# Cross network on one core: a second Strassen level for product 4 in both tiles, the W block's residual by DMA, weight loads held by deadlines

## The chip, the core and the metric

The kernel runs on one core of one Trainium2 chip. The time is in device microseconds, from the start of the execution to its end. The kernel before took 2218.09 us (median of 3 runs, 2217.39 to 2218.19). The execution that the profiler recorded took 2217.99 us, 0.1 us under that median; its instructions span 2216.2 us.

## The reference

Six layers of a cross network on a batch of 16384 rows with 1024 features, all in bfloat16:

```python
B, F, D, L = 16384, 100, 16, 6          # Din = 1024
def reference(x0, ws, bs):
    x = x0
    for l in range(L):
        proj = jnp.einsum('bd,de->be', x, ws[l]) + bs[l]
        x = x0 * proj + x
    return x
```

So each layer is one product of the state with a 1024 x 1024 weight matrix, a bias, a multiplication with the input x0, and a residual addition to the state.

## The kernel before, in words

**Tiles and units.** The batch is cut into 16 tiles of 1024 rows (`pr`), worked on in 8 groups of two (`grp`). Within a group the two tiles take turns: layer 0 of the first tile (`lane` 0), layer 0 of the second (`lane` 1), layer 1 of the first, and so on. One tile in one layer is a *unit*; there are 96, and a name such as `T1@50` is operation T1 of unit 50. Features lie on the 128 partitions, rows on the free axis. A tile has four blocks of 512 features x 512 rows, so that a block is 128 partitions x 2048 elements (`QD`). The input is in `x0Ts`, the state in `xsts`, three of each: the tiles of one group use two, the third is the one that the next group's first tile will use.

**The product.** Each unit's 1024 x 1024 x 1024 product is made by the Winograd form of Strassen's method: seven products of 512 x 512 x 512, numbered 1 to 7, with four sums of the state's blocks (`T1` to `T4`) ahead of them and the sums of weight blocks (`5`, `6`, `7`, `3`) made once in group 0 and kept in device memory (`Lc`). A product can be done in two ways. *Plain* (`group`, matmul at line 318): 4 groups of 4 matmuls, each 128 x 128 weights by 512 columns, then 4 evictions from PSUM with bias by ScalarE (line 337). *With a second level* (`inner`, matmul at line 507): seven products of half the size, `Xp1` to `Xp7`, each 4 matmuls by 256 columns. For it VectorE makes sums of quarter blocks first (`Xt13`, `Xt2`, `Xt4` into `tin`), ScalarE does seven evictions without bias (`e_p5`, `f1`, `e_c11`, `f2`, `e_u0`, `e_u1`, `e_c21`, line 327), and VectorE adds the intermediate (`Xcc`). Products 5, 2 and 3 have the second level in nearly every unit. Product 4 has it where `lane in K4[l]`: in both tiles at layer 0, in the second tile alone at layers 1 to 4, in neither at layer 5. The first tile of group 0 (`one`) has it nowhere but for product 5, as its weight sums are only being made.

**After the products.** The results lie in seven blocks of SBUF, `ev` (`P1s`, `P5s`, `Q`, `U`, `V`, `W`, `C3`), which change places from unit to unit (`home`, `NEXT`). VectorE adds them up (`Q1`, `Ua`, `Ub`, `Va`; with the second level of product 4 also `Wa`, as then V has to be added to W), multiplies each of Q, U, V, W with its block of x0 (`Qm` to `Wm`), and the residual is added: at layers 1 to 4 by an accumulating DMA that GpSimd issues for Q, U and V (`Qx`, `Ux`, `Vx`; line 564, set by `DMA_RES`), and by a VectorE addition for W. In group 0 W goes by DMA too. At layer 5 all four are VectorE additions; at layer 0 the multiplication writes the state. Every VectorE operation is recorded by the one helper at line 204.

**Weights.** They stream through a ring of 12 buffers (`wring`, tiles `wp`). From group 1 on each layer loads 11 blocks of 512 KB (10 at layer 5), on SyncE's queue (line 247), in the order of `ring_seq`: three raw blocks from `ws` and the rest from `Lc`. `pump()` runs after every operation that is emitted and issues a load as soon as the buffer that it overwrites has had its last use. On the same queue go the transposing loads of x0 (line 342) and, for the output, a transpose out of the state (line 662) and a store (line 671).

**The order of the work.** TensorE's order in a unit is written out by hand, as one of the lists `PE_FIRST`, `PE_ONE5` (first tile of group 0), `PE_TWO` (product 4 plain), `PE_FOUR` (product 4 with the second level) and `PE_LAST`. The function `schedule` then places all other operations: it is a list scheduler with a fixed cost for each operation, which gives an engine the operation whose latest start is the earliest. Costs: a VectorE operation n/1920 + 0.068 us, an eviction 0.571 us with bias and 0.475 us without, an accumulating DMA `ACCUM` = 9.0 us until its block may be read. The instructions are emitted in that order; on the chip each engine runs its own list and waits on semaphores.

Of the kernel before, what the change touches and what calls it, by code (L numbers as in the profile page):

```python
# [9 lines left out]
ADD = mybir.AluOpType.add  # L10
# [6 lines left out]
PE_FIRST = """  # L17
t0.0 t0.1 t0.2 t0.3 P1.1 bT P1.0 t1.0 t1.1 t1.2 t1.3 P1.2 P1.3 t2.0 t2.1 P2.1 t2.2 t2.3 P2.0 P2.2 P2.3
P5.1 P5.0 P5.3 P5.2 P6.3 P6.2 P6.0 P7.3 P6.1 P7.0 P4.3 P7.2 P7.1 P4.0 P4.2 P4.1 P3.0 P3.1 P3.3 P3.2
""".split()  # L20
PE_ONE5 = """
P1.1 P1.0 P2.1 P6.0 P2.0 P1.2 5p5 5p1 P1.3 P6.1 5p2 P2.3 5p6 P6.2 P2.2 5p7 P6.3 5p3 P7.2 P7.3 5p4 P3.3 P7.1 P3.2 P7.0
P4.3 P4.2 P4.0 P3.1 P4.1 P3.0
""".split()
PE_TWO = """
5p5 P1.1 5p1 P1.0 P1.3 5p2 2p5 5p6 2p1 P1.2 5p3 2p2 5p7 2p6 P6.0 5p4 2p3 3p5 2p7 3p1 P6.1 2p4 3p2 3p6 P6.2 P6.3 3p3
3p7 P7.0 P7.1 P7.2 3p4 P7.3 P4.1 P4.0 P4.3 P4.2
""".split()
PE_FOUR = """
5p5 P1.0 5p1 2p5 2p1 P1.1 5p2 5p6 2p2 P1.2 2p6 P1.3 5p3 5p7 2p3 2p7 P6.0 3p5 5p4 2p4 P6.1 P6.3 3p1 4p5 P6.2 4p1 3p2  # L30
P7.0 4p2 3p6 4p6 P7.1 3p3 4p3 4p7 P7.2 3p7 4p4 P7.3 3p4
""".split()
PE_LAST = """
# [5 lines left out]

ACCUM = 9.0  # L40

# [84 lines left out]


@with_exitstack
def kernel(
# [7 lines left out]
    nc = tc.nc  # L137
    P = nc.NUM_PARTITIONS
    B, D = x0.shape
    L = ws.shape[0]  # L140
# [10 lines left out]
    NDUMMY = 8  # L151
    K4 = {0: (0, 1), 1: (1,), 2: (1,), 3: (1,), 4: (1,)}
    DMA_RES = {1: "QUV", 2: "QUV", 3: "QUV", 4: "QUV"}

# [20 lines left out]
    EV = {"5c": P5s, "3c": C3, "U": U, "V": V, "W": W, "Q": Q, "P1s": P1s}  # L175
    NEXT = {"5c": "3c", "3c": "5c", "U": "W", "V": "U", "W": "V", "Q": "Q", "P1s": "P1s"}
    home = {r: r for r in EV}
    TURNED, rows = ((0, 0), (1, 0), (0, 1)), (P1s, U, V)
# [42 lines left out]
    for gl in range(NGROUP * L):  # L221
        if gl < L:
            ring_seq += [(gl, w, "load") for w in RAW] + [(gl, w, "make") for w in MADE]
        else:
            ring_seq += [(gl, w, "load") for w in "1 5 5i 2 2i 6 3 3i 7 4 4i".split()[:11 if gl % L in K4 else 10]]
    slot = {(gl, w): f"slot{i % RING}" for i, (gl, w, _) in enumerate(ring_seq)}
# [11 lines left out]

    def pump():
        while pos["next"] < len(ring_seq):  # L240
            gl, w, kind = ring_seq[pos["next"]]
            if kind == "make":
                return
            t = ring_tile((gl, w))
            if t is None:
                return
            nc.sync.dma_start(t[:], w_src(gl % L, w))
            pos["next"] += 1
# [29 lines left out]
    for u, (pr, l) in enumerate(units):  # L278
        one, first, last = plain(u), u == 0, u == NU - 1
        if not first:  # L280
            home = {r: home[NEXT[r]] for r in home}
        P1s, P5s, Q, U, V, W, C3 = (EV[home[r]] for r in ("P1s", "5c", "Q", "U", "V", "W", "3c"))
        CB = {"5": P5s, "2": Q, "3": C3, "4": W}
        gl, grp, lane = gl_of(u), pr // 2, pr % 2
        x0T, xst = x0Ts[pr % 3], xsts[pr % 3]
# [7 lines left out]
        ISW = [ISN[w] for w in ISLOT] + [f"is.{w}.{i}" for w in ISLOT for i in "5637"] if pr == 2 else []  # L293
        line = {w: i for i, w in enumerate(PE_FIRST if first else PE_LAST if last else PE_ONE5 if one else PE_FOUR if lane in K4.get(l, ()) and pr > 0 else PE_TWO)}

# [3 lines left out]
        def act(name, fn, rd, wr, biased_=False, u=u, occ=None):  # L299
            occ = occ or (0.571 if biased_ else 0.475)  # L300
            op(f"{name}@{u}", "ACT", occ, occ + 0.17, fn, rd, wr)
# [11 lines left out]
        def group(name, w, bank, bname, rhs, rname, m, start, gl=gl, kmajor=kmajor):  # L313
            def fn():
                for k in range(KH):
                    r = rhs[:, k, :] if kmajor else rhs[:, :, k, :]
                    o = bank[:] if kmajor else bank[:].rearrange("p (j r) -> p j r", r=P)
                    nc.tensor.matmul(o, lhsT=wt[(gl, w)][:, k, m * P:(m + 1) * P], rhs=r,  # L318
                                     start=(start and k == 0), stop=(k == KH - 1), skip_group_check=True)
            if first and name in ("P5.0", "P5.1"):  # L320
                rname = rname + ["w0.5a"]
            else:
                rname = rname + wname(w)
            pe(name, 0.863, fn, rname, [bname], [w], at={"1": ARRIVE["w0.1"], "2": ARRIVE["w0.2"]}.get(w, 0.0) if first else 0.0)
# [25 lines left out]
        def fence(q, sp, u=u):  # L350
            def fn():
                nc.gpsimd.dma_start(seen[:], x0Ts[sp][0:1, q[1], q[0] * KH, 0:32])
            op(f"fence@{u}", "POOL", 0.6, 0.6, fn, [f"x0.{sp}.{q[0]}{q[1]}"], ["xbar"])

        if l == 0 and lane == 1:
# [121 lines left out]
        if inn:  # L477
            for X, a, b in (("5", 0, 1), ("2", 2, 3), ("3", 0, 1), ("4", 2, 3))[:len(inn)]:
# [12 lines left out]
                def inner(i, bank, start, X=X, gl=gl, q=q, tk=tk, src=src, kmajor=kmajor):  # L491
                    quad = {1: (0, 0), 2: (1, 0), 3: (1, 1)}
                    rhs = (lambda k: q(*quad[i], k)) if i in quad else (lambda k: tk({4: 3, 5: 0, 6: 2, 7: 1}[i], k))
                    rn = {1: src, 2: src, 3: src, 4: X + "t4", 5: X + "t13", 6: X + "t2", 7: X + "t13"}[i]
                    w = X if i in (1, 2, 4) else X + "i"

                    def fn():
                        if i in (1, 2, 4):
                            k0, e0 = {1: (0, 0), 2: (KQ, 0), 4: (KQ, HQ)}[i]
                            wv = wt[(gl, w)][:, k0:k0 + KQ, e0:e0 + HQ]  # L500
                        else:
                            wi = weight(gl, w) if gl < L else weight(gl, w)[:]
                            wv = wi.rearrange("p q (k e) -> p q k e", k=KQ)[:, {5: 0, 6: 1, 3: 2, 7: 3}[i]]
                        for m in range(KQ):
                            for k in range(KQ):
                                o = pX[bank][:, m * NQ:(m + 1) * NQ]
                                nc.tensor.matmul(o if kmajor else o.rearrange("p (j r) -> p j r", r=P), lhsT=wv[:, k, m * P:(m + 1) * P],  # L507
                                                 rhs=rhs(k), start=(start and m == 0 and k == 0), stop=(k == KQ - 1), skip_group_check=True)
                    if gl < L and w.endswith("i"):
                        dep, wl = [f"is.{w}.{({5: '5', 6: '6', 3: '3', 7: '7'})[i]}", ISN[w]], []  # L510
                    else:
                        dep, wl = ([] if X in "24" else wname(w)), [w]
                    pe(X + f"p{i}", 0.436, fn, [rn, Xn[bank]] + dep, [Xn[bank]], wl)
# [34 lines left out]
        if not last:  # L548
            if not one:
                ttop("Q1", Q[:], Q[:], P1s[:], ADD, allm("Q") + allm("P1s"), allm("Q"))  # L550
            ttop("Ua", U[:], U[:], P5s[:], ADD, allm("U") + allm("5c"), allm("U"))
            if not one:
                ttop("Ub", U[:], U[:], C3[:], ADD, allm("U") + allm("3c"), allm("U"))
            if "4" in inn:
                ttop("Wa", W[:], W[:], V[:], ADD, allm("W") + allm("V"), allm("W"))
            ttop("Va", V[:], V[:], P5s[:], ADD, allm("V") + allm("5c"), allm("V"))
            for nm, C, q in (("Q", Q, (0, 0)), ("U", U, (0, 1)), ("V", V, (1, 1)), ("W", W, (1, 0))):
                if l == 0:
                    ttop(nm + "m", xblk(xst, *q), C[:], x0j(*q), MULT, allm(nm) + [X0[q]], [XO[q]] + ISW)
                    continue  # L560
                ttop(nm + "m", C[:], C[:], x0j(*q), MULT, allm(nm) + [X0[q]], allm(nm))
                if nm in DMA_RES.get(l, "") or nm == "W" and grp == 0 and 0 < l < L - 1:
                    def acc(C=C, q=q, xst=xst):
                        nc.gpsimd.dma_start(xblk(xst, *q), C[:], accum_op=ADD)  # L564
                    op(f"{nm}x@{u}", "POOL", 1.0, ACCUM, acc, allm(nm) + [XO[q], "xbar"], [XO[q]])
                else:
                    ttop(nm + "x", xblk(xst, *q), C[:], xblk(xst, *q), ADD, allm(nm) + [XO[q]], [XO[q]])
        else:
# [7 lines left out]
            r0 = pr * PR  # L576
            END = NU * 22.95
            half = lambda s, h: [f"{s}.{2 * h}", f"{s}.{2 * h + 1}"]
# [95 lines left out]

    order, start, _ = schedule(ops)

    ctx.enter_context(tc.manual_schedule(
# [31 lines left out]

    held = [i for i in order if ops[i].name.startswith("ld") and ops[i].name.endswith(".1@1")]  # L710
    for i in held:
        ops[i].fn()
    for i in order:
        if i not in held:
            ops[i].fn()
        for k in ops[i].weights:
            if k in uses_left:
                uses_left[k] -= 1
        pump()

# [29 lines left out]
```

## Time and profile before

| | |
|---|---|
| median of 3 runs | 2218.09 us |
| the profiled execution | 2217.99 us, span 2216.2 us |
| TensorE (PE) busy | 2203.0 us, 99%, 14637 matmuls |
| VectorE (DVE) busy | 2143.7 us, 97%, 2539 instructions |
| ScalarE (ACT) busy | 2038.9 us, 92%, 3657 instructions |
| GpSimd (POOL) busy | 211.1 us, 10%; 200 accumulating DMAs |
| DMA queue q1 (SyncE's), q0 (GpSimd's) | 53.5% and 29.1% of the 16 DMA engines' time |

An engine's busy time is the union of its instructions' spans. A span holds the start of the pipeline and its end, so that two instructions that follow each other closely overlap by some 0.09 us; the step from start to start is then shorter than the duration that a row gives. The queues' shares are of the time of all 16 DMA engines over the span.

### The profile page before, as it was taken

How to read it: one execution, taken by the hardware profiler on the slowest of the kernel's cores; microseconds unless marked ns; L12 is line 12 of the kernel's file. 1: busy time of each engine (PE TensorE's matmuls, PEld its weight loads, DVE VectorE, ACT ScalarE, POOL GpSimd, SP SyncE). 2: the span in 40 equal slices, each digit the busy share in tenths (PEclk: the TensorE clock that was granted, in tenths of full speed). 3: DMA queues.
4: the chain of work that ended last, by engine and by line, in shares of the span. 5: the costliest groups of instructions: out<-in, count | busy, mean ns of one | idle time of the engine just before them, and what ended most of it. 6: DMA issues, size and time to landing. Idle time of an engine off the chain costs nothing.

```text
span 2216.2 us, 39701 instructions
## 1 busy us (share of the span) xinstructions
PE 2203.0 (99%) x14637; PEld 1432.6 (65%) x14685; DVE 2143.7 (97%) x2539; ACT 2038.9 (92%) x3657; POOL 211.1 (10%) x271
## 2 busy tenths in 40 slices
PE   9999999999999999999999999999999999999998
PEld 5555666666666666666666666666666666666664
DVE  8999999999999999999999999999999999999997
ACT  7888899999999999999999999999999999999997
POOL 1132100110001100011000110011100111001110
PEclk9999999999999999999999999999999999999999
DMA  8788999768986689866898678976789777896777
GB/s 257 208 222 239 215 239 263 182 171 216 259 254 176 177 226 252 256 173 179 237 251 237 172 197 226 261 222 177 214 224 251 216 181 224 214 272 185 201 224 166
DMA packets 455460, 482.88 MB, mean 218 GB/s; under 512 B 269152, under 2 KB 381280, under 8 KB 455264
## 3 DMA queue, kind: packets, MB, share of 16 engines
q1 hardware_dynamic: 418352, 349.49, 53.5%
q0 software_dynamic: 36320, 130.57, 29.1%
q8 instruction: 115, 1.88, 0.3%
q14 instruction: 81, 0.66, 0.1%
q10 hardware_dynamic: 592, 0.27, 0.0%
HBM read 252.72 MB, written 58.20 MB: 140 GB/s over the span
## 4 chain that ended last, share of the span: by engine, by line
PE 99%; SPq 0%; DMA 0%; issue 0%; DVE 0%; DVEq 0%
PE pA L318 52%; PE pX L507 44%; PE pX L318 2%; DMA x0T<-in_x_dram 0%; SPq L691 0%; PE pA L611 0%; SPq L698 0%; DVE T L204 0%; SPq L704 0%; PE pX L611 0%; DVE xst L623 0%; SPq L701 0%; DVEq L204 0%
## 5 line engine op out<-in xcount | busy, mean ns | idle before, releaser
L507 PEld LDWEIGHTS <-wp 128*128 128x128 bf16 x8484 | 829.8, 98 | 275.4 <-issue 1.0
L337 ACT ACTIVATE ev<-pA,b_all 128x512 bf16<-128x512 f32 x1291 | 881.6, 692 | 107.5 <-PE pA L318 66.3
L318 PE MATMUL pA<-T,wp 128*128 128x512 bf16 x3825 | 922.2, 379 | 1.6
L318 PEld LDWEIGHTS <-wp 128*128 128x128 bf16 x5648 | 552.0, 98 | 478.4 <-issue 2.1
L327 ACT CAST ev<-pX 128x512 bf16<-128x512 f32 x1284 | 699.5, 595 | 24.2 <-PE pX L507 21.1
L507 PE MATMUL pX<-ti,wp 128*128 128x256 bf16 x4768 | 661.2, 273 | 0.0
L204 DVE TENSOR_TENSOR ev<-ev,ev 128x2048 bf16<-128x2048 bf16 x419 | 503.4, 1219 | 43.9 <-ACT ev L327 35.8
L204 DVE TENSOR_TENSOR ev<-ev,x0T 128x2048 bf16<-128x2048 bf16 (+1 forms) x324 | 386.0, 1210 | 2.3 <-ACT ev L337 1.2
L327 ACT COPY pX<-pX 128x512 f32<-128x512 f32 x638 | 370.8, 593 | 3.6
L318 PE MATMUL pA<-xst,wp 128*128 128x512 bf16 x1280 | 320.5, 379 | 0.0
L564 POOL DMA_DIRECT2D xst<-ev x200 | 172.3, 862 | 1296.8 <-ACT ev L337 445.6
L507 PE MATMUL pX<-xst,wp 128*128 128x256 bf16 x1736 | 260.5, 273 | 0.0
L507 PE MATMUL pX<-T,wp 128*128 128x256 bf16 x1628 | 244.3, 273 | 0.0
L204 DVE TENSOR_TENSOR ev<-ev,ip 128x1024 bf16<-128x1024 bf16 x319 | 214.4, 690 | 0.0
L204 DVE TENSOR_TENSOR T<-xst,T 128x2048 bf16<-128x2048 bf16 x160 | 195.6, 1223 | 1.0 <-PE pX L507 1.0
L204 DVE TENSOR_TENSOR T<-xst 128x2048 bf16<-128x2048 bf16 x160 | 195.6, 1223 | 0.0
L327 ACT CAST ip<-pX 128x512 bf16<-128x512 f32 x319 | 187.8, 589 | 2.1 <-PE pX L507 2.1
L204 DVE TENSOR_TENSOR xst<-ev,xst 128x2048 bf16<-128x2048 bf16 x116 | 141.8, 1224 | 0.1
L204 DVE TENSOR_TENSOR ti<-T,ti 128x512 bf16<-128x512 bf16 x282 | 119.6, 424 | 0.0
L204 DVE TENSOR_TENSOR ti<-xst 128x1024 bf16<-128x1024 bf16 x148 | 102.3, 691 | 9.3 <-PE pX L507 8.3
L204 DVE TENSOR_TENSOR ti<-xst,ti 128x1024 bf16<-128x1024 bf16 x148 | 101.8, 688 | 0.1
L204 DVE TENSOR_TENSOR ti<-T 128x1024 bf16<-128x1024 bf16 x141 | 97.3, 690 | 0.0
(57 smaller groups left out, 702.7 us busy)
## 6 DMA issues: line engine op xcount, KB each, us to landing
wp<-Lc SPq DMA_DIRECT2D x329, 512.0 KB, 6.1
xst<-ev POOLq DMA_DIRECT2D x200, 512.0 KB, 5.3
wp<-in_ws_dram SPq DMA_DIRECT2D x148, 512.0 KB, 6.7
out_dram<-x0T SPq DMA_DIRECT2D x60, 512.0 KB, 4.3
Lc<-wp POOLq DMA_DIRECT2D x24, 512.0 KB, 5.9
Lc<-xst POOLq DMA_DIRECT2D x23, 512.0 KB, 8.9
ev<-in_x_dram SPq DMA_DIRECT2D x3, 512.0 KB, 6.5
wp<-in_ws_dram SPq DMA_DIRECT2D x4, 256.0 KB, 7.4
```

Of the source, the lines that this page charges most:

```text
L204: nc.vector.tensor_tensor(out=o, in0=a, in1=b, op=op)
L318: nc.tensor.matmul(o, lhsT=wt[(gl, w)][:, k, m * P:(m + 1) * P], rhs=r, start=(start and k == 0), stop=(k == KH - 1), skip_group_check=True)
L327: act(name, lambda: nc.scalar.copy(out=dst, in_=src), rd, wr)
L337: act(name, lambda: nc.scalar.activation(out=dst, in_=src, func=IDENT, bias=b_all[:, c:c + 1], scale=1.0), rd, wr, True)
L507: nc.tensor.matmul(o if kmajor else o.rearrange("p (j r) -> p j r", r=P), lhsT=wv[:, k, m * P:(m + 1) * P], rhs=rhs(k), start=(start and m ...
L564: nc.gpsimd.dma_start(xblk(xst, *q), C[:], accum_op=ADD)
```

## The change

- **Product 4.** `K4` now names both tiles for layers 0 to 4. The first tile takes the second level for product 4 at layers 1 to 4 as well (in groups 1 to 7).
- **W's residual.** `DMA_RES` is "QUVW" at layers 1 to 4: the VectorE addition `Wx` becomes an accumulating DMA in all groups.
- **The idle state tile.** In groups 1 to 7 the second tile's Q, U, V and W of layers 1 to 4 are no longer in `ev` but in the third state tile, which the next group's first tile does not need before its layer 0 (`S` names). An operation `lend`, which emits no instruction, puts this in order with the output transposes that read the tile before and with the writes of the next group's layer 0. The places in `ev` change by another cycle (`NEXT`).
- **Loads.** `LOAD_ORDER` replaces the order of the blocks in the ring. After scheduling, `plan_loads` gives each load of groups 1 to 7 a time: not before its buffer is free, laid out one after the other with 1.45 us a load and 2.9 us for each accumulating DMA that it lets pass, and no later than 7.0 us ahead of its first use (less where several are due in a row). `pump` holds a load until that time has come in the order of emission, and the load then waits for the newest matmul emitted by then.
- **Orders and costs.** `PE_ONE5` (now `PE_ONE_INNER`), `PE_TWO` and `PE_FOUR` are other permutations of the same entries; `Ua` is recorded after `Wa`; the costs are 0.583 and 0.482 us for evictions and 9.5 us for an accumulating DMA, and the due time of the last outputs is `NU * 22.8`.

```diff
-ACCUM = 9.0
+ACCUM = 9.5
+LOAD, BURST, LEAD, GRACE = 1.45, 2.9, 7.0, 4.0
+LOAD_ORDER = "1 5i 2i 5 2 6 3i 3 4i 4 7".split()
...
+def plan_loads(loads, bursts):
+    deadline, nxt = [0.0] * len(loads), 1e9
+    for n in range(len(loads) - 1, -1, -1):
+        nxt = min(nxt, loads[n][1] - LEAD)
+        deadline[n] = nxt
+        nxt -= 1.3 * LOAD
+    issue, t, b = [], 0.0, 0
+    bursts = [s + 1.0 for s in sorted(bursts)] + [1e9]
+    for (free, _), due in zip(loads, deadline):
+        while True:
+            t = max(t, min(free, bursts[b]))
+            if bursts[b] <= t and (free > t or bursts[b] + GRACE <= due):
+                t += BURST
+                b += 1
+            else:
+                break
+        issue.append(t)
+        t += LOAD
+    return issue
...
-    K4 = {0: (0, 1), 1: (1,), 2: (1,), 3: (1,), 4: (1,)}
-    DMA_RES = {1: "QUV", 2: "QUV", 3: "QUV", 4: "QUV"}
+    K4 = {l: (0, 1) for l in range(L - 1)}
+    DMA_RES = {l: "QUVW" for l in range(1, L - 1)}
...
-    NEXT = {"5c": "3c", "3c": "5c", "U": "W", "V": "U", "W": "V", "Q": "Q", "P1s": "P1s"}
+    NEXT = {"5c": "Q", "3c": "5c", "U": "V", "V": "W", "W": "U", "Q": "3c", "P1s": "P1s"}
...
-    def pump():
+    def pump(time=0.0):
         while pos["next"] < len(ring_seq):
             gl, w, kind = ring_seq[pos["next"]]
-            if kind == "make":
+            if kind == "make" or held.get((gl, w), 0.0) > time:
                 return
...
-            nc.sync.dma_start(t[:], w_src(gl % L, w))
+            ld = nc.sync.dma_start(t[:], w_src(gl % L, w))
+            if (gl, w) in held:
+                tc.add_manual_dep(ld.ins, newest["pe"].ins.name, mybir.DependencyInfo(mybir.DependencyClass.Sync, mybir.DependencyReason.DATA))
...
+        idle = (2 * grp + 2) % 3
+        home = dict(cycle)
+        if grp > 0 and lane and 0 < l and not last:
+            home.update({r: "S" + r for r in "QUVW"})
+        EV.update({"S" + r: xsts[idle][:, i // 2, i % 2] for i, r in enumerate("QUVW")})
...
+        if lane == 0 and (grp > 0 and l == 1 or grp > 1 and l == 0 or grp == NGROUP - 1 and l == L - 1):
+            state = pr % 3 if l == 0 else idle
+            op(f"lend@{u}", "POOL", 0.0, 0.0, lambda: None, (), [f"S{r}.{m}" for r in "QUVW" for m in range(KH)] + [f"xs.{state}.{a}{b}" for a, b in QD])
...
-                if nm in DMA_RES.get(l, "") or nm == "W" and grp == 0 and 0 < l < L - 1:
+                if nm in DMA_RES.get(l, ""):
...
+    plan = plan_loads([(free_at[ring_seq[n - RING][:2]], first_use[k]) for n, k in late_keys],
+                      [start[i] for i, o in enumerate(ops) if o.name[1:3] == "x@" and o.eng == "POOL"])
+    for (_, k), t in zip(late_keys, plan):
+        held[k] = t
...
-        pump()
+        pump(start[i])
```

## The prediction

> **What bounds the kernel now.** I read the page's busy times first, then who waited for whom on TensorE and VectorE, then the chain of waits with its starts, then a table by stretches, one stretch for the two units of a layer, in group 4 (layers 0 to 5), and last the DMAs' landing times. From the page:
>
> ```profile
> PE 2203.0 (99%) x14637; PEld 1432.6 (65%) x14685; DVE 2143.7 (97%) x2539; ACT 2038.9 (92%) x3657; POOL 211.1 (10%) x271
> q1 hardware_dynamic: 418352, 349.49, 53.5%
> q0 software_dynamic: 36320, 130.57, 29.1%
> PE 99%; SPq 0%; DMA 0%; issue 0%; DVE 0%; DVEq 0%
> L507 PEld LDWEIGHTS <-wp 128*128 128x128 bf16 x8484 | 829.8, 98 | 275.4 <-issue 1.0
> ```
>
> A busy PE alone proves nothing, since the ends of matmuls are modelled. But the waits of PE between 300 and 2150 us are an empty list, and the chain's starts show the pace (start, length, then the number of matmuls):
>
> ```profile
> 1220.92 4.32 PE pA L318 x20
> 1226.54 1.31 PE pX L507 x12
> ...
> 1266.49 4.32 PE pA L318 x20
> ...
> 1357.63 4.32 PE pA L318 x20
> ...
> 1380.61 4.32 PE pA L318 x20
> ```
>
> A plain matmul takes 4.32 / 20 = 0.216 us, a half-width one 1.31 / 12 = 0.1092 us. The runs of 20 end the units with a plain product 4: two units of layers 1 to 4 take 1266.49 - 1220.92 = 45.57 us, a unit of layer 5 takes 1380.61 - 1357.63 = 22.98 us. So the unit with product 4 in two levels takes 45.57 - 22.98 = 22.59 us. TensorE sets the end at every point; the others only have to keep up. How closely they do is in the stretches (span, busy PE, PEld, DVE, ACT, POOL, clock, DMA share, GB/s):
>
> ```profile
> 1111.40:1156.50 45.10, 44.79 (x314) 31.09 (x319) 45.10 (x55) 43.27 (x80) 0.51 (x1) 1.00 0.99 254
> 1156.50:1202.20 45.70, 45.70 (x311) 30.23 (x310) 45.47 (x55) 43.04 (x78) 3.48 (x4) 1.00 0.92 251
> 1202.20:1247.80 45.60, 45.60 (x311) 30.16 (x309) 43.89 (x52) 42.75 (x78) 5.13 (x6) 1.00 0.73 200
> 1293.40:1339.00 45.60, 45.60 (x310) 30.16 (x309) 43.90 (x52) 42.76 (x78) 5.16 (x6) 1.00 0.73 196
> 1339.00:1384.90 45.90, 45.90 (x298) 28.89 (x297) 44.65 (x50) 41.98 (x75) 2.24 (x3) 1.00 0.83 201
> ```
>
> The first line is the one to remember: at layer 0 both tiles already run product 4 in two levels, DVE has no gap at all, and PE keeps its pace (the missing 0.3 us are missing records; it waited for nothing). The granted clock is 1.00 throughout.
>
> **TensorE, the only gain.** Converted are the first tiles of groups 1 to 7 at layers 1 to 4: 28 units. Each loses 16 plain matmuls (16 x 0.216 = 3.456 us) and gets 28 half-width ones (28 x 0.1092 = 3.058 us): 0.40 us. The units' lengths say 22.98 - 22.59 = 0.39. I take 0.395 x 28 = 11.1 us; the ends are 10.9 and 11.2. The 336 more weight loads take 98 ns each, less than the 109 ns of the matmul that covers them, as in the 8484 of that row. New orders of the same entries cost TensorE nothing while no entry waits; the start (to the first dense stretch) and the tail do the same work as before.
>
> [...]
>
> **ScalarE.** Per converted unit four evictions with bias go and seven without come. In a dense piece the steps from start to start are 0.59 us (1234.83 to 1235.42) and 0.46 to 0.51 us; 28 x (7 x 0.48 - 4 x 0.59) = 28 us more, 2067 of some 2205. Per pair it comes to layer 0's 43.27 of 45.10, with PE unhindered. Cost 0.
>
> **VectorE.** Steps from start to start, from the timeline: three 2048-element operations take 1344.02 - 1340.62 = 3.40 us, so 1.135 each; 1024 elements take 0.60; 512 take 0.335 (the row's 0.424 less the same 0.09 of overlap). A converted unit adds 4t13 and 4cc (1.20), 4t2 and 4t4 (0.67) and Wa (1.135): 3.01 us, 84.3 in all. W's residual leaves VectorE in 56 units (two tiles, four layers, seven groups): -63.6. Net +20.7 us in a time that is 11.1 shorter: 2164.4 of 2205, 98.2%; idle time shrinks from 72.5 to 40.7. Per pair of layers 1 to 4: 43.9 + 3.01 - 2.27 = 44.6 of 45.2. Lower end of the cost: 0, as all of it lies beside PE (layer 0's line, which has the same list of operations). Upper end: all 72.5 us of idle time are forced by dependences and stay; then VectorE sets the end and the time grows by the 20.7. I take 0, because layer 0's line is the same work at the same rate, and it is entered there with the backlog of layer 5, which stays as it is (four VectorE residuals, 44.65 of 45.90).
>
> **W by DMA.** 56 more accumulating DMAs of 512 KB. Queue q0's 29.1% is 645 us for 200 of them and 50 plain ones; the plain ones at the pace of q1's 4 KB packets (1.42 us a block, by the packets) leave 2.87 us each. So +160 us: the DMA engines go from 83% to about 91%, and a pair of layers 2 to 4 from 0.73 to 0.73 + 2 x 2.87 / 45.4 = 0.86. Nobody waits for a share; T1, 2t13, T2 and 3t13 of the same tile's next unit wait for landings:
>
> ```profile
> DMA to landing us min/median/max: 4.5/5.3/11.7
> ...
> xst<-ev POOLq DMA_DIRECT2D x6, 512.0 KB, 4.8
> ...
> xst<-ev POOLq DMA_DIRECT2D x9, 512.0 KB, 6.3
> ```
>
> These are all 200; then one pair of layer 2 in group 4 with six; then 208 to 254 us, in group 0, where W goes by DMA already and eight saves of weights run beside it. Even there the median is 6.3, against the 9.5 us that the order of work now allows and the 9.0 that it allowed. On GpSimd nothing waits behind an accumulation but the next (0.86 us each, 48 us more of an engine at 10%). Lower end 0; upper end 11.7 - 9.5 = 2.2 us of wait in each of 56 units, less the 40 us of idle, +83 us. I take 0, from group 0's row, which is nearest in kind: four per unit, DMA share 0.90 there, 0.4 us of wait for a landing on VectorE, none on PE.
>
> [...]
>
> **Held loads.** No load is added. What changes is when it is issued: as late as 7.0 us ahead of its use where the DMA engines have no other cause to take it earlier, and it first waits for a group of 4 matmuls to end, which costs up to 0.86 us of that. SyncE is in order, so behind a held load wait the next load, the transposes of x0 and the outputs; and PE waits for the load. Rows:
>
> ```profile
> wp<-Lc SPq DMA_DIRECT2D x329, 512.0 KB, 6.1
> ...
> wp<-in_ws_dram SPq DMA_DIRECT2D x148, 512.0 KB, 6.7
> ...
> DMA to landing us min/median/max: 3.2/6.3/13.2
> ```
>
> The medians come from bursts: five loads issued between 1232.2 and 1236.1 landed from 1238.4 to 1244.8, one every 1.3 to 2.4 us, behind an accumulation. Laid out 1.45 us apart, with 2.9 us left for accumulations (both the trace's own 1.42 and 2.87), they should be nearer 3.2 to 6. Lower end 0; the upper end is a rival below. I take 0.
>
> **Idle state tile.** It adds no instruction. The second tile's evictions no longer write blocks that the first tile's accumulations read; ScalarE shows no wait for those now, so nothing is gained. A new wait is for the output transposes that empty that tile: the last is over by 1155.5 us in group 4 (GpSimd's fence), the second tile's layer 1 begins after 1179. Cost 0. `Ua` behind `Wa`: same work.
>
> **Sum.** 2217.99 - 11.1 = 2206.9 for an execution like the profiled one; the median of the runs stood 0.1 above it, so 2207.0.
>
> **Rivals.**
> *Held loads land late (slower).* At the 35 stretches of layers 1 to 5 in groups 1 to 7 the 7 us less up to 0.86 are all there is. If the worst load of each stretch lands 1.2 us late (8.2 us; about a tenth of the loads take that now), PE stops for it: 35 x 1.2 = 42, to 2249 us. It turns at 11.1 / 35 = 0.32 us a stretch. For it: today PE never meets a load, so the margin is untested. Against it: the spacing, and the shortest landing of 3.2.
> *The same, in part.* Some 0.1 to 0.2 us a stretch, or a few late landings of W: 3 to 7 us of the gain go, 2210 to 2214.
> *VectorE becomes the bound.* Its idle time stays at 72.5 us: 2218.0 + 20.7 = 2238.7. It turns where the idle time falls by less than 20.7, to 51.8. For it: 98.2%, and 44 us of today's idle time between 300 and 2150 us are waits, 34 of them for ScalarE's evictions. Against it: they come at some 1.2 us a stretch in layers 2 to 5, where VectorE runs ahead, and layer 0 has none.
> *Half-width matmuls are paced by their weight loads.* 98 ns under 109: the rows exclude it.
>
> **How the numbers follow.** A difference under 0.2% (4.4 us) can hardly be told from none here. Dense PE, 2206 to 2209: 0.72. Gain eaten in part: 0.11 (2209 to 2213.7). Late loads: 0.06 within 0.2%, 0.07 slower. VectorE bound: 0.04, slower. Paced by weight loads: none. So faster 0.83, same 0.06, slower 0.11. The range is 2205.5 (the 11.2 and a little less tail) to 2213.7; it leaves the last three cases out.
>
> **What would show it.** Right: 22.6 us for every unit of layers 1 to 4, still no waits of PE between 300 and 2150, DVE without gaps (about 45 of 45.2) in layers 1 to 4, 256 accumulations at line 564's successor with a median near 6 us, q0 at about 36%. Wrong: waits of the weight loads on `wp`, or of PE on `ti` and `T` with DVE waiting for the landing of `xst`.

## The result, and the profile after

The changed kernel takes 2299.36 us (median of 6 runs, 2292.77 to 2311.91) and the kernel before 2217.77 us (median of 6): a ratio of 1.0376, 95% interval 1.0342 to 1.0411. It is 81.6 us slower; 2207.0 us had been forecast. The profiled execution of the changed kernel took 2293.25 us, near the fast end of its runs; its instructions span 2291.4 us, 75.2 us more than the span of before. Against those 75.2 us the accounts below are made.

From the page of the changed kernel, its busy times, its two large queues and the chain's shares by engine:

```profile
PE 2212.4 (97%) x14973; PEld 1468.8 (64%) x15021; DVE 2173.3 (95%) x2623; ACT 2058.0 (90%) x3741; POOL 259.1 (11%) x327
q1 hardware_dynamic: 418352, 349.49, 54.2%
q0 software_dynamic: 44384, 159.94, 34.2%
PE 82%; DMA 11%; DVE 5%; issue 1%; ACT 1%; SPq 0%; POOLq 0%; ACTq 0%; DVEq 0%
```

Before, TensorE was 99% busy and 99% of the chain. Now DMAs are 11% of the chain and VectorE 5%: the end is set in many places by something that arrives late. TensorE's waits between 300 and 2150 us, an empty list before (what waited, for what: us in all, times, the longest):

```profile
PE pA L351 <- DMA wp<-Lc: 29.0, 18, 3.1
PE pX L544 <- ACT pX L360: 13.9, 12, 3.0
PE pX L544 <- DMA wp<-in_ws_dram: 8.8, 5, 3.5
PE pA L351 <- DVE T L228: 5.3, 2, 2.8
PE pX L544 <- ACT ev L370: 0.7, 1, 0.7
```

The weights (`wp`) come late most often, and ScalarE's evictions next. Group 4 by stretches, layers 0 to 4, with the columns of the table shown of before (span, busy PE, PEld, DVE, ACT, POOL, clock, DMA share, GB/s):

```profile
1146.20:1193.30 47.10, 45.21 (x317) 31.33 (x321) 47.10 (x56) 43.06 (x81) 0.50 (x1) 1.00 0.98 255
1193.30:1238.50 45.20, 45.20 (x323) 31.29 (x321) 44.96 (x56) 43.05 (x82) 4.33 (x5) 1.00 0.88 221
1238.50:1283.60 45.10, 45.10 (x322) 31.21 (x320) 44.89 (x56) 43.47 (x81) 6.87 (x8) 1.00 0.88 224
1283.60:1330.40 46.80, 45.44 (x323) 31.30 (x322) 45.98 (x56) 43.66 (x81) 6.88 (x8) 1.00 0.88 215
1330.40:1379.90 49.50, 46.98 (x323) 31.90 (x321) 44.91 (x55) 43.80 (x81) 6.91 (x8) 0.97 0.82 205
```

Layers 1 and 2 run as forecast: 45.1 to 45.2 us a stretch instead of 45.6, TensorE without a gap, 44.9 us of VectorE, a DMA share of 0.88. Layers 0, 3 and 4 of the same group do not: 47.1, 46.8 and 49.5. In the last the granted clock is 0.97. So the steady state that was forecast exists, and what costs is how often it is broken.

**One late load.** The chain of the changed kernel around 1580 us (start, length, what):

```profile
1576.68 1.75 PE pX L544 x16
1578.43 0.88 PE pA L351 x4
1579.32 9.75 DMA wp<-Lc
1589.12 1.04 PE pA L351 x4
```

On SyncE's timeline (start, time on the queue) this load was the fifth since 1571; on GpSimd's, two accumulations were issued within 1.3 us of it:

```profile
1571.08 6.10 SPq L273 DMA_DIRECT2D wp<-Lc  x3
1578.02 0.38 SPq L273 DMA_DIRECT2D wp<-in_ws_dram  x1
1579.32 0.32 SPq L273 DMA_DIRECT2D wp<-Lc  x1
```
```profile
1578.33 0.86 POOL L602 DMA_DIRECT2D xst<-xst  x1 [10.17 <-ACT ev L360]
1580.61 0.86 POOL L602 DMA_DIRECT2D xst<-xst  x1 [1.41 <-ACT ev L360]
```

Those accumulations landed after 8.9 and 9.7 us, the load after 9.75. TensorE wanted it 6.8 us after its issue and stood for 3.0 us.

**One late x0.** The second kind of stop is at layer 0. In the waits between 1425 and 1450 us one delay is handed on three times, from a transposing load of x0 to VectorE, to ScalarE and to TensorE:

```profile
DVE T L228 <- DMA x0T<-in_x_dram: 4.6, 1, 4.6
...
PE pX L544 <- ACT pX L360: 3.6, 2, 3.0
ACT ip L360 <- DVE ev L228: 3.3, 1, 3.3
```

VectorE waits there for the last of the first tile's four transposes, which was issued at 1417.67 and landed at 1425.73. SyncE's timeline ahead of it shows why it is late: the transposes hold the queue for 2 to 4.6 us each, and loads stand between them:

```profile
1403.84 7.17 SPq L375 DMA_TRANSPOSE x0T<-in_x_dram  x3
1412.21 0.33 SPq L273 DMA_DIRECT2D wp<-Lc  x1
1412.63 3.88 SPq L375 DMA_TRANSPOSE x0T<-in_x_dram  x1
1416.62 0.53 SPq L273 DMA_DIRECT2D wp<-Lc  x1
1417.23 0.38 SPq L273 DMA_DIRECT2D wp<-in_ws_dram  x1
1417.67 4.64 SPq L375 DMA_TRANSPOSE x0T<-in_x_dram  x1
```

The kernel before starts earlier: in six of seven groups it issues the first of these four 13.2 to 13.6 us ahead of the first `T1` of their tile, the changed kernel 9.2 to 10.1 us.

**The account.** I took every step from the start of one matmul to the start of the next and called what it has over 0.216 us (0.109 for half width) a stop, where that is over 0.25 us. Stops make 69.1 us: 46.0 on late loads (26 stops of 0.5 to 3.7 us), 17.4 behind ScalarE, 5.6 behind VectorE. Another 13.7 us go at half clock: 27 us with a granted clock of 0.50, in windows of 3.4 us, each about the end of a stop of 2.6 to 3.7 us. The part after the last product's matmul grew from 9.7 to 14.5 us (last section). What is left, span less stops, half clock and end:

| | span | stops | half clock | end | left |
|---|---|---|---|---|---|
| before | 2216.2 | 0.0 | 0.0 | 9.7 | 2206.5 |
| changed | 2291.4 | 69.1 | 13.7 | 14.5 | 2194.1 |

The difference in the last column is some 12 us; 11.1 were forecast for TensorE. In the versions with few stops (below) it is 10.7 to 11.4. The gain is there, and 88 us of other losses lie on it.

### The profile page after: what moved, and what is told of

Same layout as the page of the kernel before. It is cut to its first block, busy times and chain, and to the rows that moved or that the text cites. A ratio compares the mean times of both kernels' runs of the same rounds, so it can differ in the third digit from the quotient of the medians.

```text
span 2291.4 us, 40900 instructions
## 1 busy us (share of the span) xinstructions
PE 2212.4 (97%) x14973; PEld 1468.8 (64%) x15021; DVE 2173.3 (95%) x2623; ACT 2058.0 (90%) x3741; POOL 259.1 (11%) x327
## 3 DMA queue, kind: packets, MB, share of 16 engines
q1 hardware_dynamic: 418352, 349.49, 54.2%
q0 software_dynamic: 44384, 159.94, 34.2%
## 4 chain that ended last, share of the span: by engine, by line
PE 82%; DMA 11%; DVE 5%; issue 1%; ACT 1%; SPq 0%; POOLq 0%; ACTq 0%; DVEq 0%
PE pA L351 40%; PE pX L544 39%; DMA wp<-Lc 8%; PE pX L351 2%; DVE xst L228 2%; DMA wp<-in_ws_dram 2%; DVE T L228 1%; DVE ti L228 1%; DVE ev L228 1%; DMA x0T<-in_x_dram 1%; DMA xst<-xst 0%; ACT pX L360 0%; SPq L739 0%; DMA xst<-x0T 0%; ACT ev L370 0%
## 5 line engine op out<-in xcount | busy, mean ns | idle before, releaser
L351 PE MATMUL pA<-T,wp 128*128 128x512 bf16 x3377 | 847.2, 381 | 39.6 <-DMA wp<-Lc 32.7
L544 PE MATMUL pX<-ti,wp 128*128 128x256 bf16 x5216 | 723.1, 273 | 0.0
L370 ACT ACTIVATE ev<-pA,b_all 128x512 bf16<-128x512 f32 x883 | 603.7, 694 | 112.5 <-PE pA L351 84.0
L360 ACT CAST ev<-pX 128x512 bf16<-128x512 f32 x1148 | 644.3, 594 | 25.5 <-PE pX L544 13.3
L360 ACT COPY pX<-pX 128x512 f32<-128x512 f32 x694 | 394.5, 590 | 14.8 <-PE pX L544 11.4
L228 DVE TENSOR_TENSOR ev<-ev,ev 128x2048 bf16<-128x2048 bf16 (+1 forms) x283 | 338.9, 1209 | 19.2 <-ACT ev L370 11.9
L228 DVE TENSOR_TENSOR ev<-ev,x0T 128x2048 bf16<-128x2048 bf16 (+2 forms) x188 | 223.9, 1192 | 0.4
L370 ACT ACTIVATE xst<-pA,b_all 128x512 bf16<-128x512 f32 x296 | 203.6, 688 | 19.3 <-PE pA L351 9.1
L228 DVE TENSOR_TENSOR xst<-xst,ev 128x2048 bf16<-128x2048 bf16 x136 | 165.5, 1218 | 1.6 <-ACT ev L360 0.6
L228 DVE TENSOR_TENSOR xst<-xst,x0T 128x2048 bf16<-128x2048 bf16 x136 | 164.3, 1216 | 0.2
L602 POOL DMA_DIRECT2D xst<-xst x112 | 96.2, 859 | 550.7 <-ACT ev L360 343.9
```

The costliest lines, as they stand in the source:

```text
L228: nc.vector.tensor_tensor(out=o, in0=a, in1=b, op=op)
L351: newest["pe"] = nc.tensor.matmul(o, lhsT=wt[(gl, w)][:, k, m * P:(m + 1) * P], rhs=r, start=(start and k == 0), stop=(k == KH - 1), skip_ ...
L360: act(name, lambda: nc.scalar.copy(out=dst, in_=src), rd, wr)
L370: act(name, lambda: nc.scalar.activation(out=dst, in_=src, func=IDENT, bias=b_all[:, c:c + 1], scale=1.0), rd, wr, True)
L544: newest["pe"] = nc.tensor.matmul(o if kmajor else o.rearrange("p (j r) -> p j r", r=P), lhsT=wv[:, k, m * P:(m + 1) * P], rhs=rhs(k), sta ...
```

## The experiments

After the result three explanations stood against each other. By the first the deadline of 7 us is too short by itself. By the second the fourth accumulation a unit crowds the DMA engines, so that whatever is issued late, or behind others, lands late. By the third VectorE, at 98%, has no room left and makes the delays. The runs undo one part, do one part alone, or take work away from one suspect.

### One part at a time

The changed kernel with its loads issued as soon as their buffers are free, as before the change:

```diff
-    for (_, k), t in zip(late_keys, plan):
-        held[k] = t
+    held.clear()
```

> The changed kernel whole, but its loads are issued as before, as soon as their buffer is free; no load waits for a matmul. Theory A (holding the loads to some 7 us ahead of use is what costs): the waits of PE and of its weight loads on wp go, the clock stays at 1.00, and the time falls from 2299 to 2207 to 2214 us. Theory B (the 56 more accumulating DMAs load the DMA engines so that loads come late however they are issued): it stays at 2270 or more, with PE still waiting for wp.

Measured: 2284.08 us, ratio 1.029 (1.0269 to 1.031). The late loads are gone and the kernel is hardly faster, so neither theory holds as it was written. Its waits, of TensorE and then of VectorE (300 to 2240 us):

```profile
PE pX L544 <- ACT pX L360: 32.8, 29, 3.0
PE pX L544 <- DVE ti L228: 16.3, 19, 1.4
...
DVE ti L228 <- DMA xst<-ev: 41.0, 24, 3.7
DVE T L228 <- DMA x0T<-in_x_dram: 20.6, 6, 5.2
```

Now it is the accumulations that land late: VectorE waits 41.0 us for the state, 20.6 for x0. Loads issued early take the DMA engines' time ahead of them: the median landing of a load is 7.2 and 11.0 us (5.1 and 6.0 when held), and a tenth of the accumulations out of `ev` take over 11.3 us (8.4 when held). The same shortage shows at another place. And it reaches W itself: with the accumulations taken in the order in which the kernel issues them, 30.8 us of the waits for the state are for the first tile's W, whose accumulations in groups 1 to 7 land after 11.2 us in the median, where the order of work allows 9.5. The late x0 is here too, though no load is held.

The other two parts, each put alone into the kernel before. Held loads alone (`plan_loads`, `held` and `pump(start[i])` as in the change, the load order of before):

```diff
-        pump()
+        pump(start[i])
```

> The kernel before with nothing changed but the hold (the same rule, 7 us, its own order of loads). Theory A: stops on wp of some 0.5 us a layer or more though the accumulations are still 200: 2225 to 2260 us. Theory B: 2218 us, as the DMA engines have no more to do than before.

Measured: 2228.41 us, 1.0054 (1.0039 to 1.0069), with 9.4 us of stops, 8.7 of them on `wp`. So held loads are sometimes late even at three accumulations a unit, with a fifth of the stops of the changed kernel. It is not a test of the same margin, though. In the schedule that each kernel's own code makes, the 7 us rule puts 79 of the 455 held loads of the changed kernel less than 8 us ahead of their first use (the shortest 6.9), and here none (the shortest 8.7). W by DMA alone:

```diff
-    DMA_RES = {1: "QUV", 2: "QUV", 3: "QUV", 4: "QUV"}
+    DMA_RES = {l: "QUVW" for l in range(1, L - 1)}
```

> The kernel before with nothing changed but W's residual by DMA in all groups (256 accumulations, loads as early as before). Theory A: 2218 us, PE without waits, the DMA engines at some 90%. Theory B: loads and landings late, 2240 us or more.

Measured: 2231.26 us, 1.0061 (1.0045 to 1.0078). This moves 56 additions off VectorE, whose busy time falls from 2143.7 to 2092.5 us, and still the kernel is slower: 7.3 us of stops behind ScalarE, 4.2 us more at the end, and a wait that before did not have, all of it for the first tile's U, whose accumulations now take 8.9 us in the median instead of 7.2:

```profile
DVE T L204 <- DMA xst<-ev: 22.3, 27, 2.5
```

Alone, then, held loads cost 10.7 us, W by DMA 13.5, and product 4 gains 11.1 by the forecast: +13 us if they added up. Together they cost 81.6. No run has product 4, the order of the loads, the idle state tile or the new orders of work alone; but all of these are also in the version of 2215.93 us below, so by themselves they don't cost 80 us. The loss lies in how the parts meet. The late x0, too, comes neither with held loads alone nor with W by DMA alone: VectorE never waits for it in these two kernels.

### Is it the crowding?

The accumulations are cut to half their bytes, once with early loads and once with the 7 us of the change:

```diff
-                        nc.gpsimd.dma_start(xblk(xst, *q), C[:], accum_op=ADD)
+                        nc.gpsimd.dma_start(xblk(xst, *q)[:, 0:KQ], C[:, 0:KQ], accum_op=ADD)
```

> The changed kernel without the hold (2284 us), each accumulating DMA carrying only the first half of its block, so that half of every residual at layers 1 to 4 is left out; instructions and waits are the same. Theory B and E (crowded DMA engines, landings later than the order of work allows): landings back to some 4 to 6 us, 2206 to 2216 us, the rest being x0 at layer 0. Theory D alone (a full VectorE, whatever the landings): 2250 us or more.

> The changed kernel, loads held to 7 us as in it, but each accumulating DMA adds only the first half of its block (256 KB instead of 512; the other half of the residual is left out). It tells whether the loads of 7 us are late by themselves or through the accumulations. Theory D (the accumulations crowd the DMA engines): some 190 us of engine time go, more than W by DMA brought, and the 46 us of PE's stops on wp fall below 10; with the layer-0 stops that remain, 2225 to 2240. Theory M (7.0 us less the wait for a matmul is too little margin by itself, whatever runs beside it): stops on wp stay above 30 us, 2270 or more. The kernel of before with held loads at 7 us, three accumulations a unit, had 8.7 us of them.

Measured: 2238.24 us, 1.0093 (1.0078 to 1.0108), with early loads (2284.08 with whole accumulations) and 2242.6 us, 1.011 (1.0097 to 1.0124), with held ones (2299.36). The second kernel's waits of TensorE:

```profile
PE pX L544 <- ACT pX L360: 12.6, 7, 3.0
PE pA L351 <- DMA wp<-Lc: 9.8, 11, 1.8
PE pX L544 <- DMA wp<-in_ws_dram: 0.8, 3, 0.4
```

The stops on loads fall from 46.0 to 13.5 us with not a load issued at another time by the plan. That is much nearer to the crowding's "below 10" than to the "above 30" of a margin that is too short by itself, though not below 10, and the time lies 2.6 us above the crowding's range: 7 us costs something even so. What the cut leaves in both kernels is the late x0 of layer 0: TensorE waits 17.6 us (early loads) and 12.6 us (held) behind ScalarE. So x0 is late with early loads and with light accumulations as well: neither held loads nor whole accumulations are what makes it late.

Is VectorE the one that has no room? One addition of 1.135 us in 95 units is left out of the kernel with early loads:

```diff
-            ttop("Ua", U[:], U[:], P5s[:], ADD, allm("U") + allm("5c"), allm("U"))
```

> The changed kernel without the hold (2284 us), and without the addition Ua in all units but the last, so that U lacks product 5; VectorE has 1.1 us less in each unit, some 93 instead of 98% of the time. Theory D (late landings cost only because VectorE has no idle time to absorb them): 2210 to 2235 us. Theory E (the next unit's sums must wait for the landing whatever VectorE has left): 2260 us or more, with VectorE still waiting for the landing of xst.

Measured: 2251.61 us, 1.0159 (1.0142 to 1.0176). The time lies between the two forecasts. Some 108 us less work on VectorE bring 32.5 us, half of what this kernel loses against the one before; and VectorE, at 92%, still waits 63 us for the state to land (48.9 for `ti`, 14.2 for `T`). It passes delays on because it has little slack to absorb them; the waits themselves are for DMAs. Its load is part of the price even so: the kernel before with W by DMA, at 94%, has early loads and four whole accumulations too and loses 13.5 us.

### When to load

The changed kernel with 12 us instead of 7:

```diff
-LOAD, BURST, LEAD, GRACE = 1.45, 2.9, 7.0, 4.0
+LOAD, BURST, LEAD, GRACE = 1.45, 2.9, 12.0, 4.0
```

> The changed kernel with a deadline of 12 us ahead of the first use in place of 7. Theory A: loads land in 5 to 10 us, so nearly all stops go: 2210 to 2235 us, with a few waits on wp left where the buffer itself comes free late. Theory B: 2270 or more, since the DMA engines carry the same traffic.

Measured: 2237.04 us, 1.0089 (1.0072 to 1.0106), 2 us above the range of theory A. Stops on `wp` fall from 46.0 to 1.1 us. The 16.3 that stay are the late x0: VectorE's `T` waits 19.7 us for it. Next, the plan also leaves room for the four transposes of each first tile's x0:

```diff
-                      [start[i] for i, o in enumerate(ops) if o.name[1:3] == "x@" and o.eng == "POOL"])
+                      [start[i] for i, o in enumerate(ops) if o.name[1:3] == "x@" and o.eng == "POOL"]
+                      + [start[i] - 2.0 for i, o in enumerate(ops) if o.name[:2] == "ld" and o.name[5:].split("@")[0] in [str(p) for p in range(0, NPAIR, 2)]])
```

> The changed kernel with the 12 us deadline (2237 us), and in addition layer 0's weight loads let the first tile's four x0 transposes pass on SyncE, as they let accumulations pass. Theory C (what is left at 12 us is x0 coming late behind weight loads once a group, at a VectorE that is too full to make it up): VectorE's 20 us of waits for x0T go, with them the stops of about 3 us at layer 0 and their slow clock: 2212 to 2222 us. Rival (the stops come from the full VectorE alone, x0 late or not): 2232 us or more.

Measured: 2215.93 us (median of 10, 2213.47 to 2218.85), 0.9993 (0.9983 to 1.0002): two edits of the plan take 83 us back. TensorE's waits and its stretches of group 4, layers 0 to 3, now:

```profile
PE pA L351 <- DMA wp<-Lc: 0.8, 1, 0.8
PE pX L544 <- DMA wp<-in_ws_dram: 0.7, 1, 0.7
PE pX L544 <- ACT pX L360: 0.3, 1, 0.3
```
```profile
1108.70:1154.30 45.60, 45.45 (x322) 31.27 (x320) 45.60 (x55) 42.98 (x80) 0.50 (x1) 1.00 0.99 276
1154.30:1199.50 45.20, 45.20 (x322) 31.30 (x321) 44.96 (x57) 43.05 (x82) 4.33 (x5) 1.00 0.86 223
1199.50:1244.70 45.20, 45.20 (x323) 31.34 (x322) 44.99 (x56) 43.57 (x81) 6.87 (x8) 1.00 0.88 223
1244.70:1289.90 45.20, 45.20 (x323) 31.34 (x321) 44.99 (x56) 43.57 (x81) 6.88 (x8) 1.00 0.87 228
```

VectorE's busy time is 2165.5 us, the same work as in the changed kernel, at 98% of the span. What is left of span after stops (3.0), half clock (0.0) and the end (14.6) is 2195.8: 10.7 us under the kernel before.

The control, 12 us in the kernel before with held loads, and the room for x0 with the old 7 us:

> The kernel before with nothing changed but the hold, at 12 us in place of 7 (which gave 2228). If only the short deadline costs: 2217 to 2220 us and no waits on wp. If issuing loads behind matmuls costs in itself (SyncE in order, loads pushed into the accumulations): 2224 us or more.

> The changed kernel (7 us) with nothing added but that the first tile's x0 transposes go ahead of layer 0's weight loads. Theory F (two separate losses in the changed kernel: x0 late at layer 0, and weight loads late at 7 us): VectorE's wait for x0T and the stops at layer 0 go, about 20 us with the slow clock, and the waits on wp stay: 2265 to 2285 us. Rival (the loads' deadline alone): 2295 us or more.

Measured: 2222.07 us, 1.0021 (1.0012 to 1.003), between the two forecasts: holding brings nothing there at either of the two times. And 2295.56 us, 1.0337 (1.0312 to 1.0361): a miss of my sum. The stops for x0 are gone, as meant, but those on loads grew from 46.0 to 62.1 us, and half clock from 13.7 to 29.0. (The profiled execution took 2304.78 us, the longest of the four, and may overstate the growth.) Why they grew no run shows. These two losses, in any case, could not be taken away one at a time.

Then the time itself, with room for x0: 16, 10, and 13 (the last with the saves moved as below).

```diff
-LOAD, BURST, LEAD, GRACE = 1.45, 2.9, 12.0, 4.0
+LOAD, BURST, LEAD, GRACE = 1.45, 2.9, 16.0, 4.0
```

> As the run at 2216 us (12 us, x0 first), with 16 us in place of 12. If its last stops on wp and the clock lost after them are what is left: 2209 to 2214 us, below the kernel before. If the loads, now earlier, crowd the accumulations instead: 2218 to 2235 us, with VectorE waiting for xst.

> The same kernel of 2215.9 us with LEAD 10 instead of 12 (7 gave 2295.6, 16 gave 2250.6). Theory P (the loads' landings have a tail up to some 11 us at four accumulations a unit): 5 to 20 us of stops on wp return, 2222 to 2245. Theory Q (a broad optimum between 7 and 12): 2212 to 2217.

> The kernel with the saves on SyncE (2215.2 us) with LEAD 13 instead of 12. Loads a little earlier: the last late loads (0.8 us of stops on wp) go, but the accumulations are crowded a little more. Theory R (the side of the late loads is steep, that of the early ones flat near 12: LEAD 10 gave 2244.9, 16 gave 2250.6): 2211 to 2214, faster than before by over 0.15%. Theory S (12 is the bottom of a narrow valley): 2217 to 2226.

| LEAD, us | 7 | 10 | 12 | 13 (saves moved) | 16 |
|---|---|---|---|---|---|
| median, us | 2295.56 | 2244.9 | 2215.93 | 2227.04 | 2250.57 |
| stops on `wp`, us | 62.1 | 29.5 | 1.9 | 3.4 | 1.3 |
| waits of VectorE's `ti` for accumulations out of `ev`, us | 0.5 | 3.7 | 5.1 | 7.6 | 21.8 |

A valley: on one side loads are late, on the other accumulations are, and x0 with them (9.5 and 11.6 us of waits at 13 and 16). At 13 I had hoped for a version ahead of both kernels; it is 11 us behind 12. 16 is worse than both forecasts for it, 2209 to 2214 and 2218 to 2235 us.

### Holding only layer 0's loads

The kernel of 2215.93 us, with the loads of the other layers free, with whole and with half accumulations:

```diff
-        held[k] = t
+        if k[0] % L == 0:
+            held[k] = t
```

> No hold but for layer 0's weight loads, which let the x0 transposes pass (12 us deadline there). Theory F without a hold leaves the landings late behind early loads (VectorE waiting for xst, some 40 us): 2240 to 2265 us. Rival (without a hold x0 is all that is lost): 2225 us or less.

> No hold but for layer 0's weight loads, and each accumulating DMA carries only the first half of its block, so that half of the residuals of layers 1 to 4 is left out. With both causes of theory F gone (x0 late, crowded landings) TensorE should run at its full pace on the changed work: 2206 to 2212 us. If a VectorE at 98% is a cause of its own: 2220 us or more.

Measured: 2266.72 us, 1.0217 (1.0202 to 1.0232). From VectorE's waits of this kernel:

```profile
DVE ti L228 <- DMA xst<-ev: 55.9, 25, 3.7
```

So x0 is in time, and at layers 1 to 4 early loads crowd the accumulations: 52.2 us of VectorE's waits for the state are for the first tile's W. With half accumulations the same kernel takes 2214.29 us (median of 10), 0.9983 (0.9974 to 0.9992), 2 us above the better forecast: with the bytes goes the loss, and no load of layers 1 to 5 needs to be held. Early loads live beside three whole accumulations in the kernel before and beside four halves here, but not beside four whole ones. Its stops are 2.8 us, and 2195.1 us are left of its span, the 2206.5 of before less 11.4.

### The end

GpSimd's last instruction of note is a `DRAIN`, and it took 5.30 us before, where GpSimd had issued 264 DMAs, and 9.77 us in the changed kernel with 320. In the version with 12 us and room for x0, the saves of the weight sums in group 0 are issued by SyncE:

```diff
-                    nc.gpsimd.dma_start(Lc[l, CIDX[w]].rearrange("p (k e) -> p k e", k=KH), t())
-                op(f"s{w}@{u}", "POOL", 1.0, 7.0, fn, rd + (["gate"] if u == 0 else []), (), [(gl, x) for x in weights])
+                    nc.sync.dma_start(Lc[l, CIDX[w]].rearrange("p (k e) -> p k e", k=KH), t())
+                op(f"s{w}@{u}", "SP", 1.0, 7.0, fn, rd + (["gate"] if u == 0 else []), (), [(gl, x) for x in weights])
```

> The kernel with loads held to 12 us and room for the x0 transposes (2215.9 us), with the saves of the weight sums in group 0 issued on SyncE's queue instead of GpSimd's, so that GpSimd issues some 270 DMAs instead of 320. Theory N (GpSimd's last DRAIN is longer the more DMAs GpSimd has issued): the DRAIN falls from 10.0 to 5.5 us and the end with it, 2211.5 to 2213.5, faster than before by over 0.2%. Theory O (the DRAIN's length has to do with the accumulations, 256 for 200): it stays near 10 us, 2215 to 2217. Should the saves, now in SyncE's order, hold back loads in group 0, stops of PE ahead of 300 us would show it and add to either.

Measured: 2215.24 us (median of 11, 2211.26 to 2221.08), 0.9991 (0.9982 to 1.0000). With 273 DMAs, of which as before the move 256 are accumulations, the DRAIN took 7.61 us: shorter, but not by the count alone, which would have put it near the 5.30 of 264. What sets it stays open. In the profiled executions the end fell from 14.6 to 11.7 us; of that only 0.7 us show in the medians. This is the lowest median of a version that does the whole work, and it can't be told from the kernel before.

## Why the prediction was wrong

**TensorE, 11.1 us: right.** Undisturbed stretches of layers 1 to 4 take 45.1 to 45.2 us, 22.6 a unit, and the spans without stops, half clock and end differ by 10.7 to 11.4 us (three versions with under 5 us of stops). Half-width matmuls were not paced by their weight loads: a load takes 98 ns in the changed kernel, and 16 of the matmuls behind each other 1.75 us, 109 ns each.

**VectorE and ScalarE: right in amount, and not the bound.** Forecast 2164.4 us, 98.2%; the version with 12 us and room for x0 has 2165.5 us at 98%, and TensorE keeps its pace. ScalarE has 2055.6 there, for some 2067. But a VectorE with 41 us of idle time in 2200 passes every late landing on, and the forecast used "no cost" for it as if its inputs stayed as punctual as they had been.

**W by DMA, "I take 0": the step that failed.** The share of the DMA engines was right (0.86 forecast for a pair of layers 2 to 4, 0.88 measured; the whole kernel's "about 91%" adds up to 89, and to 90 in the version with 12 us and room for x0). The bounds were not, for they asked only what W's landing costs those who wait for W. In the changed kernel that is small (3.6 us of waits of `ti` for `xst<-xst`, all of them for the second tile's W). The cost there is with others that share the 16 DMA engines, the weight loads above all: cut the accumulations' bytes by half and 32.5 of the 46.0 us of stops on loads go. With early loads the first bound fails too, as W itself lands late (11.2 us where 9.5 are allowed). Alone in the kernel before it is 13.5 us, outside any number that was given for the likeliest case. The row of group 0 was the wrong neighbour: it has four accumulations a unit and a DMA share of 0.90 too, but only five weight loads pass in its 46 us, where a layer has eleven from group 1 on, and no load there is held to a deadline.

**Held loads, "I take 0": the other step that failed.** The landing times did fall, as the forecast said: from 6.1 and 6.7 to 5.1 and 6.0 us. From the page of the changed kernel (KB each, median us to landing):

```profile
wp<-Lc SPq DMA_DIRECT2D x329, 512.0 KB, 5.1
wp<-in_ws_dram SPq DMA_DIRECT2D x148, 512.0 KB, 6.0
xst<-ev POOLq DMA_DIRECT2D x144, 512.0 KB, 7.1
xst<-xst POOLq DMA_DIRECT2D x112, 512.0 KB, 8.1
```

But a margin is held against the tail. A tenth of the loads still take over 7.2 us from `Lc` and over 8.4 from `ws`, the longest 12.2 and 16.9, and 6.1 to 7.0 us were all that the forecast allowed for the tightest. The argument went from the median of a changed distribution, and it spaced the loads by 1.45 and 2.87 us as if they took turns with the accumulations; the late load above shared nearly its whole time with two of them. (The change's description has one thing the wrong way round: where several loads are due in a row, `plan_loads` sets the earlier ones' deadlines further ahead of their use, not less.)

**The rival *Held loads land late*** had this mechanism, its place and nearly its price: 42 us forecast as 35 stretches of 1.2, 46.0 measured in 26 stops of 1.8 on average. That the product came so near is luck: there were fewer stops than it counted, and each was longer. The other losses, some 42 of 88 us, it did not have. It was given a chance of 0.07 as a slower kernel. What speaks against giving it so little was already in its own text: that loads of 8.2 us were not rare (about a tenth, it said; 7% by the trace of before), and that the turning point was 0.32 us a stretch. "Against it: the spacing" was not a row, but a hope about a plan. The sign that the forecast named for being wrong, weight loads that wait on `wp`, is the first line of TensorE's waits above.

**Not foreseen:** the late x0 at layer 0, some 16 us; the half clock behind long stops, 13.7 us; and 4.8 us at the end. The forecast named x0 as waiting behind held loads and gave that no price. But holding is not what makes it late: VectorE waits 25 us for x0 with early loads, 12.6 in the changed kernel, and nothing in the kernel before with held loads (7 or 12 us) or with W by DMA. It comes with a part of the change that no run isolates, in which the transposes also start 3 to 4 us later against layer 0; letting the loads stand back for them cures it.

## What to carry to other kernels

Put alone into the kernel before, W's additions took the DMA engines from 83 to 90% busy and cost 13.5 us, though the forecast found nobody who would wait for their result: ask who else's transfers share the engines, and hold each deadline against the slowest tenth of the landings (7.2 and 8.4 us here), not the median (5.1 and 6.0). A prefetch has two wrong times, too late for its reader and too early for the others, and in a kernel with three engines over 90% the room between them was here narrower than 3 us (2244.9 us at 10 and 2227.04 at 13, against 2215.93 at 12). Price a long stop of TensorE at more than its length: in the changed kernel seven of the eleven stops of 2.6 us or more had 3.4 or 6.8 us with a granted clock of 0.50 about their end, by which 13.7 us were lost in all.

## What the runs showed of the hardware that was not expected

**Half clock in the middle of a dense kernel.** In the changed kernel the trace has a granted clock of 0.50 at 399.8 us for 6.8 us, and at 1017.6, 1068.8, 1348.7, 1447.7, 1918.7 and 2198.6 us for 3.4 us each, each within 1.3 us of the end of a stop of TensorE of 2.6 to 3.7 us. The one at 1447.7 follows the late x0 above (same columns as the stretches; this window, then the next):

```profile
1447.70:1451.10 3.40, 3.40 (x14) 1.82 (x12) 3.40 (x4) 2.31 (x5) 0.00 (x0) 0.50 1.15 216
1451.10:1454.50 3.40, 3.40 (x26) 2.27 (x24) 3.40 (x6) 3.11 (x6) 0.00 (x0) 1.00 1.09 286
```

Fourteen matmuls for 26. Of the eleven stops of 2.6 us or more seven had such a window and four had not, the one of 3.0 us at 1589 among them.

In this trace the seven and the four differ in how the stop lies on a grid. The seven starts are 181, 15, 82, 29, 138 and 82 times 3.413 us apart. If the trace is cut into windows by this grid, TensorE stood still for 2.15 to 3.30 us of the window ahead of each of the seven, and for 2.13 us at most in any other window of full clock: the four stops without effect were each divided between two windows, with at most 2.0 us in one. Whether the share of a window is what counts, and where a limit would lie, these stops do not show.

**Two queues, the same engines.** Loads go out on SyncE's queue and accumulations on GpSimd's. Of the time of the 16 DMA engines SyncE's queue took 54.2% and GpSimd's 34.2% over the span of the changed kernel, and 45.4% and 52.2% between 1570 and 1592 us, around the late load above. Each delays the other: halving the bytes of the accumulations took 32.5 us of stops from the loads, and issuing the loads early took the slowest tenth of the accumulations out of `ev` from 8.4 to 11.3 us.

**GpSimd's last DRAIN** lasted 5.2 to 5.4 us in the three versions with 264 DMAs issued by GpSimd, 7.6 and 8.0 in the two with 273, and 8.5 to 10.3 in the thirteen with 320. In the changed kernel the last transfer of all had landed 4.1 us before it ended (2286.5 and 2290.6 us). What it waits for was not found out.
